# Skip term inside the spectral product, shift inside the first stage of u's transform, and a new order of the work

## The chip, the cores and the metric

The kernel runs on one core of one Trainium2 chip. A core has five engines with an instruction stream each: TensorE (PE in the profile; PEld is its weight load), VectorE (DVE), ScalarE (ACT), GpSimd (POOL) and SyncE (SP). The last two mostly start DMA transfers here. The metric is the device time of one execution in microseconds. Three executions of the kernel before took 679.55, 679.65 and 680.83 us; the median is 679.65 us.

## The reference, cut to what matters

One transformer-like block with adaptive layer norms: 2048 time steps (L) of 512 channels (D). The first half is a state-space convolution (S4), done in the reference by a Fourier transform of length 4096; the second half is a dense layer of 512 to 1792 to 512 with the Mish function.

```python
mod = (_silu(c) @ w_mod).reshape(c.shape[0], 6, 1, -1)
sa, ca, ga, sb, cb, gb = ...
h = _layernorm(x) * (1 + ca) + sa
x = x + ga * S4(h)
h = _layernorm(x) * (1 + cb) + sb
x = x + gb * mlp(h)

# S4(u): K is a kernel of 2048 taps per channel, from the parameters A, B, C, dt
K = einsum("dn,dnl,dn->dl", C, exp(dt * A * l), dt * B).real
y = irfft(rfft(pad(u)) * rfft(pad(K)))[:L] + u * Dskip
```

Two terms are what the change is about: the shift `sa` that is added to the normalised input, and the skip `u * Dskip`.

## The kernel before, in words

The channels are four blocks `b` of 128. Each block has eight steps; a step of the kernel's side has the number `k` = 0 to 31, a step of the spectral side has the number `v` = 0 to 31. Two streams run beside each other and meet in a product.

**The kernel's side** makes K for 16 channels a step and transforms it. Parameters of a block are worked out on VectorE in stages (`params`, called `p0` to `p5` in the plan, tiles `raw` and `pk`). For blocks 1 to 3 the last stage, `p5`, is followed by 48 small DMAs from GpSimd (`load_s`, called `ls`, tiles `s`): 32 for the first half of the block, 16 for the second. From them TensorE makes the coarse exponents (`vt`, tile `pco`) and the angles (`ang`, tile `pang`); ScalarE takes exponentials (`va`, tiles `co`, `cf`) and sines (`sin`, tile `ec`); VectorE multiplies them (`mag`, tile `m`, and `comb`, four instructions on `ec`); TensorE contracts (`kgen`, tile `pkg`, then `ka`, tile `pka`, with ScalarE's copy `ks` between), and ScalarE copies the result to `gk` (`tm`). After eight steps a block's `gk` is whole and the second stage of its transform can be made (`ubk`, tile `pkb`, four products with the table `mf`).

**The input's side** normalises the 2048 rows (tiles `xr`), and makes the first stage of u's transform over 32 time steps at a time (`ua`, eight groups, each 8 products of 32x64 weights `bdu` into four banks `pua`). ScalarE copies the 32 banks to SBUF (`us`), SyncE stores them to DRAM in 64 transfers (`ud`). When all of it is stored, SyncE reads it back in the other layout (`gu`, one transfer a step). Second stage: `ubu` (tile `pub`, the same table `mf`), scaled by ScalarE into `ug` with the gate `gd` (`ug`). VectorE multiplies `pkb` and `ug` into `q` and adds the two halves (`prod`). Back: transpose (`t1`, tile `pt`), inverse second stage (`invb`, tile `pib`), a store and a load through DRAM, inverse first stage (`inva`, tile `pia`), and a VectorE addition onto x (`add`).

**The two terms before.** The shift is constant over time, so it is added to the spectrum as (shift / scale) times the known transform of a constant: one bf16 product `pub<-su,sab` ahead of the four `mf` products in every `ubu` (line 790). `sab` holds the ratio in three bf16 parts that VectorE and ScalarE make in turn from a broadcast (`srt`, `sra`, `srv`). The first `ubu` waits for the third `sra`. The skip is a tap at time zero of K: a product with 4 rows, `pkg<-skip`, after the 32 products of each `kgen` (line 622).

**What sets the order.** Everything from step 2 on is ordered by `_plan` (line 57), a list scheduler that runs while the program is built. Every piece of work is an `op` with an engine, a cost in `NS`, a priority from `LEAD` or `AT`, and the pieces it waits for; TensorE, ScalarE and VectorE then issue in exactly that order (class `InOrder`). A piece that is not ready holds all that stands behind it on its engine. SyncE's and GpSimd's transfers are put in place by the framework, following the same list. PSUM has six single banks that go round (`psum`, tag `pb`) and one double bank for `pang`. The last eight spectral steps stand in `drain()` in an order written by hand, and then comes the dense part.

Of the kernel before, what the change touches and what calls it, by code (L numbers as in the profile page):

```python
# [11 lines left out]
F32 = mybir.dt.float32  # L12
# [27 lines left out]
NS = {"ang": 1400, "sin": 2900, "mag": 1140, "comb": 3570, "kgen": 1130, "ks": 270, "ka": 620, "tm": 560, "ubu": 1410,  # L40
      "ug": 770, "ubk": 1020, "prod": 1760, "t1": 590, "yt": 490, "invb": 1000, "z": 500, "inva": 1060, "add": 1210,
# [4 lines left out]
LEAD = {"ang": -0.94, "sin": -10.68, "mag": 10.1, "comb": 8.65, "kgen": 0.44, "ks": -5.36, "ka": -4.53,  # L46
        "tm": 5.68, "ubu": 7.3, "ug": 3.1, "ubk": 8.28, "prod": 9.39, "t1": 7.94, "yt": 15.87, "invb": 9.41,
        "z": 10.16, "inva": 15.63, "add": 16.89}
AT = {"ua": 1.0, "un": 0.19, "nr": -0.6, "lf": 3.0, "na": 3.0, "sr": 5.0, "st": -0.5, "us": 0.0, "m3": 1,
      "m5": 2, "m0": 3, "p2": -18.07, "p3": -1.69, "pa": -0.41, "p4": -14.88, "p5": -4.69, "ls": 4.36,  # L50
      "p0": -20.55, "p1": -7.87, "v1": -14, "v2": -4.01, "v3": -4.01, "vn": 1.22, "e1": 0, "e2": 0, "e3": 0,
      "m1": 18.57, "m2": 21.11, "m4": 26.23}
# [4 lines left out]
def _plan(k0):  # L57
# [9 lines left out]
    for n, g in enumerate(UO):  # L67
# [3 lines left out]
        op(("ua", g), "T", at, [("nr", g), ("nr", 8 + g)] + ([("ua", UO[n - 1])] if n else []), 4)  # L71
# [5 lines left out]
    for n, i in enumerate((3, 5, 0)):  # L77
        at = AT[f"m{i}"]
        op(("we", i), "S", at - 1, [("mm", (3, 5, 0)[n - 1])] if n else [])
# [4 lines left out]
    op(("sr", 0), "V", AT["sr"], [("mo", i) for i in (3, 5, 0)])  # L84
# [8 lines left out]
    for k in range(max(k0 - 1, 0), nk - 1):  # L93
        op(("kgen", k), "T", lead("kgen", k), [("comb", k), ("ka", k - 1)], 2)
        op(("ks", k), "A", lead("ks", k), [("kgen", k), ("ka", k - 1)])
        op(("ka", k), "T", lead("ka", k), [("ks", k)])
        op(("tm", k), "A", lead("tm", k), [("ka", k)], frees=[("kgen", k)])
# [39 lines left out]
    for n, e, d in (("srt", "T", ("sr", 0)), ("sra", "A", ("srt", 0)), ("srv", "V", ("sra", 0)), ("sra", "A", ("srv", 1)),  # L137
                    ("srv", "V", ("sra", 1)), ("sra", "A", ("srv", 2))):
        i = d[1] + (n == "srv")
        op((n, i), e, AT["sr"], [d, ("prod", -1)], n == "srt", [("srt", 0)] if (n, i) == ("srv", 1) else None)  # L140
# [63 lines left out]
def _constants():  # L204
# [34 lines left out]
    z = np.exp(-2j * np.pi * (4 * np.arange(2048) + 1) / 8192)  # L239
    one = ((1 + 1j) / (1 - z)).reshape(64, 8, 4)  # L240
    one = np.stack([one.real, one.imag]).transpose(2, 0, 3, 1).reshape(4, 2, 512)
    su = np.zeros((4, 32, 2, 512))
    hl = np.zeros((P, 2))
    for e in range(3):
# [3 lines left out]
        for n in range(3):  # L248
            su[:, 3 * n + e] = part
            hl[3 * n + e::32, :n] = -1  # L250
    f = np.float32
    return {
        "su": su.reshape(P, 1024).astype(f),
        "hl": hl.astype(f),
# [14 lines left out]
        "tap": np.eye(4, 4, dtype=f).repeat(32, axis=1) * (np.arange(P) % 32 == 0).astype(f),  # L269
# [19 lines left out]
def s4_block(ctx, tc, io, out):  # L289
# [87 lines left out]
    skip = cst.tile([4, 2, P], F32, name="skip")  # L377
    nc.sync.dma_start(skip[:, 0], io["tap"])
    nc.sync.dma_start(skip[:, 1], io["skip"])
# [1162 lines left out]
```

## Time and profile before

| | |
|---|---|
| median of 3 runs | 679.65 us (679.55 to 680.83) |
| profiled execution, first to last instruction | 686.5 us |
| PE busy | 631.9 us, 92% |
| DVE busy | 475.4 us, 69% |
| ACT busy | 403.8 us, 59% |
| POOL busy | 101.3 us, 15% |
| granted TensorE clock, mean | 0.955 |

The profiled execution is 6.85 us longer than the median of the timed runs; the profile gives its span alone, and no other time of that execution. The profile is of one execution; its stages are: up to about 44 us loads and the first parameters; 44 to 120 us the first stage of u and the first kernel steps; 120 to 320 us the steady part, in which both streams run; 320 to 354 us the drain; then the end of the S4 half and the dense part.

How to read the rows. A row of a timeline has the start, the length, the engine, the source line (almost always 301, a helper through which all work is issued), the operation, `out<-in`, the shape and how many instructions were merged. In brackets stands idle time of the engine just before and what ended it. A row of a group ends with busy time and the mean of one instruction, then idle time before the group's instructions and what ended it. A row of windows has the stretch, its length, and for each engine the busy time in it (with the instructions), then the granted clock, the DMA share and GB/s. A matmul in fp32 shows as two records. The length of a PE row holds the emptying of the array, which the next row overlaps; what a piece costs in a row of work without gaps is the distance from its start to the start of the next.

### The profile page before, as it was taken

Reading aid. Unit: us, or ns where it says so; the run is one execution under the profiler, and the core shown is the slowest. Engines: PE = TensorE matmul, PEld = TensorE weight load, DVE = VectorE, ACT = ScalarE, POOL = GpSimd, SP = SyncE. Lnnn points to the kernel's source line nnn. Section 1 sums busy time; section 2 is a strip of 40 time slices with the busy share of each in tenths; the row PEclk is TensorE's granted clock in tenths of the full one; section 3 lists DMA queues with packets and bytes.
Section 4 is the critical chain, followed back from the end, with each engine's and each line's share of the span. In section 5 each row is a group of like instructions: output and inputs, shape, how many; then the busy total and the mean of one; then the engine's idle time right before and its main releaser. Section 6 shows DMA issues by size and latency. Waiting matters only on the chain.

```text
span 686.5 us, 16596 instructions
## 1 busy us (share of the span) xinstructions
PE 631.9 (92%) x6746; PEld 507.0 (74%) x6746; DVE 475.4 (69%) x903; ACT 403.8 (59%) x707; POOL 101.3 (15%) x212
## 2 busy tenths in 40 slices
PE   0578888999989999999999999999999999999997
PEld 0434465678868677877875888789899899998996
DVE  7988877997499986996766898476336823653233
ACT  3678769867788779876643764453445334534231
POOL 2004413542107240000100000000000001000000
PEclk9958777989999999999999999999999999999999
DMA  9968978422466466555998987667334653373332
GB/s 250 209 228 228 229 182 243 110 63 72 116 181 167 129 186 184 149 150 163 255 269 237 317 277 226 216 172 201 119 92 135 177 151 92 93 215 124 93 93 62
DMA packets 108220, 117.55 MB, mean 171 GB/s; under 512 B 12904, under 2 KB 84976, under 8 KB 106992
## 3 DMA queue, kind: packets, MB, share of 16 engines
q1 hardware_dynamic: 93296, 85.62, 44.1%
q0 software_dynamic: 14464, 30.36, 15.8%
q8 instruction: 53, 0.87, 0.6%
q10 hardware_dynamic: 384, 0.52, 0.3%
q14 instruction: 23, 0.19, 0.1%
HBM read 81.85 MB, written 32.51 MB: 167 GB/s over the span
## 4 chain that ended last, share of the span: by engine, by line
PE 68%; DVE 12%; DMA 9%; ACT 7%; issue 3%; SPq 1%; DVEq 0%; ACTq 0%
PE pr L301 25%; PE pp L301 9%; PE pkg L301 7%; PE pang L301 6%; PE pub L301 5%; PE pib L301 4%; DMA xr<-in_A_u 3%; PE pkb L301 3%; ACT ec L301 2%; PE pt L301 2%; DVE raw L301 2%; DVE ec L301 2%; PE pia L301 2%; DMA w2s<-in_B_w 1%; DVE w L301 1%
## 5 line engine op out<-in xcount | busy, mean ns | idle before, releaser
L301 PE MATMUL pr<-hh,w 128*128 128x256 f32 (+1 forms) x420 | 78.2, 327 | 0.5 <-ACT hh L301 0.5
L301 ACT ACTIVATE ec<-pang 128x1024 f32<-128x1024 f32 x64 | 62.4, 1030 | 25.3 <-PE pang L301 25.3
L301 PEld LDWEIGHTS pr<-hh,w 128*128 128x128 f32 x420 | 66.6, 188 | 12.7 <-ACT hh L301 1.9
L301 DVE TENSOR_TENSOR mh<-x,pr 128x256 f32<-128x256 f32 x63 | 26.4, 419 | 65.2 <-PE pr L301 64.9
L301 PE MATMUL pp<-w,mah 128*128 128x512 f32 x224 | 71.3, 400 | 0.0
L301 PE MATMUL pr<-w,mah 128*128 128x512 f32 x224 | 70.4, 396 | 0.0
L301 DVE TENSOR_TENSOR ec<-ec,m 128x1024 f32<-128x1024 f32 x64 | 61.3, 957 | 9.8 <-ACT ec L301 4.8
L1262 POOL DMA_DIRECT2D w<-w2d x42 | 22.2, 528 | 303.5 <-PE pp L301 197.5
L301 ACT ACTIVATE mh<-mh,b 128x256 f32<-128x256 f32 x63 | 32.1, 510 | 53.2 <-DVE mh L301 52.9
L528 POOL DMA_DIRECT2D s<-pk x96 | 47.4, 500 | 65.2 <-PE pang L301 58.6
L301 ACT ACTIVATE mh<-pr,b 128x256 f32<-128x256 f32 (+1 forms) x35 | 19.4, 559 | 63.0 <-PE pr L301 63.0
L301 DVE TENSOR_TENSOR q<-pkb,ug 128x1024 f32<-128x1024 f32 x32 | 39.1, 1221 | 22.7 <-PE pkb L301 22.5
L301 DVE TENSOR_TENSOR mal<-mh,mah 128x512 fp32r<-128x512 f32 x56 | 38.6, 689 | 15.8 <-ACT mah L301 15.7
L301 DVE TENSOR_TENSOR m<-cf 128x1024 f32<-128x1024 f32 x32 | 39.0, 1218 | 10.2 <-ACT cf L301 10.2
L301 ACT ACTIVATE ug<-pub,gd 128x512 f32<-128x512 f32 x64 | 34.0, 590 | 20.4 <-PE pub L301 20.4
L301 PE MATMUL pr<-w,mal 128*128 128x512 f32 x112 | 44.3, 395 | 0.0
L301 PE MATMUL pp<-w,mal 128*128 128x512 f32 x112 | 44.2, 394 | 0.0
L301 PEld LDWEIGHTS pkg<-ec 128*32 128x32 f32 x2048 | 35.4, 117 | 11.1 <-ACT us L301 4.4
L301 PE MATMUL pkg<-ec 128*32 128x64 f32 x2048 | 40.8, 234 | 3.0 <-ACT us L301 1.9
L301 PEld LDWEIGHTS pp<-w,mah 128*128 128x128 f32 x224 | 38.9, 191 | 5.1
L301 DVE TENSOR_TENSOR x<-x,pr 128x256 f32<-128x256 f32 x42 | 17.6, 419 | 34.3 <-PE pr L301 34.3
L526 POOL DMA_DIRECT2D s<-pk x48 | 23.7, 500 | 108.0 <-ACT ks L301 56.0
(172 smaller groups left out, 1418.2 us busy)
## 6 DMA issues: line engine op xcount, KB each, us to landing
w<-w2d POOLq DMA_DIRECT2D x42, 512.0 KB, 3.6
ud<-us SPq DMA_DIRECT2D x64, 128.0 KB, 2.7
gu<-ud SPq DMA_DIRECT2D x32, 256.0 KB, 3.2
zd<-z SPq DMA_DIRECT2D x32, 256.0 KB, 4.1
zt<-zd SPq DMA_DIRECT2D x32, 256.0 KB, 5.2
w2d<-w SPq DMA_DIRECT2D x14, 512.0 KB, 3.9
xf<-x2d SPq DMA_DIRECT2D x16, 256.0 KB, 4.7
x2d<-xp SPq DMA_DIRECT2D x14, 256.0 KB, 3.1
```

Of the source, the lines that this page charges most:

```text
L301: ins = f(*a, **kw)
L526: nc.gpsimd.dma_start(S3[b, i][q, :], pk[32 * i:32 * i + 32, 8 + k, :])
L528: nc.gpsimd.dma_start(S12[b, g][64 * e + 16 * k:64 * e + 16 * k + 16].rearrange("p h n -> p (h n)"), pk[d, k + 4 * e, :])
L1262: nc.gpsimd.dma_start(t, w2d[f])
```

## The change

1. The skip is added to the spectrum of K inside VectorE's product: `(pkb + skip) * ug`, which needs two instructions of 512 elements where one of 1024 was. The product `pkg<-skip` is gone from all 32 `kgen`. `Dskip` is loaded as 128x4 single numbers.
2. The shift is added in the first stage: the transform over 32 steps of a constant is `cs`, and each `ua` group gets 8 more products `pua<-sab,cs` (32 rows, 64 columns of weights, bf16). The product `pub<-su,sab` is gone from all 32 `ubu`. `sab` now has to be there ahead of the first `ua` instead of the first `ubu`. The ratio is split into three bf16 parts on 128x4 numbers, then broadcast by 16 small bf16 products; two ScalarE copies and two VectorE instructions of 512 elements go.
3. The gate `gd`, which needs the third slice of the modulation, is split off (`gates`, `sg`); the slices 3 and 5 load side by side into different tiles.
4. All priorities in `LEAD` and `AT` are new, and the costs of `kgen`, `ubu`, `ua`, `sra` and `sr`.

```diff
-NS = {... "kgen": 1130, ... "ubu": 1410,
+NS = {... "kgen": 1110, ... "ubu": 1010,
...
-      "sc": 2600, "nr": 450, "ua": 1150, "us": 580, "we": 240, "na": 490, "lf": 60, "sr": 400}
-LEAD = {"ang": -0.94, "sin": -10.68, "mag": 10.1, "comb": 8.65, "kgen": 0.44, "ks": -5.36, "ka": -4.53,
...
+      "sc": 2600, "nr": 450, "ua": 1400, "us": 580, "we": 240, "na": 490, "lf": 60, "sr": 1100, "sg": 200}
+LEAD = {"ang": -1.72, "sin": -14.83, "mag": 4.37, "comb": 8.2, "kgen": 8.11, "ks": 1.94, "ka": -7.81, "tm":
...
-        op(("ua", g), "T", at, [("nr", g), ("nr", 8 + g)] + ([("ua", UO[n - 1])] if n else []), 4)
+        op(("ua", g), "T", at, [("nr", g), ("nr", 8 + g)] + ([("ua", UO[n - 1])] if n else [("sra", 0)]), 4)
...
-    op(("sr", 0), "V", AT["sr"], [("mo", i) for i in (3, 5, 0)])
+    op(("sr", 0), "V", AT["sr"], [("mo", i) for i in (3, 5)])
+    op(("sg", 0), "V", AT["sg"], [("mo", 0), ("sr", 0)])
...
-        op(("ubu", v), "T", lead("ubu", v), [("gl", v, LOAD), ("ug", v - 1), ("t1", v - 2)] + ([("sra", 2)] if v == 0 else []), 1)
-        op(("ug", v), "A", lead("ug", v), [("ubu", v), ("t1", v - 2)], frees=[("ubu", v)])
+        op(("ubu", v), "T", lead("ubu", v), [("gl", v, LOAD), ("ug", v - 1), ("t1", v - 2)], 1)
+        op(("ug", v), "A", lead("ug", v), [("ubu", v), ("t1", v - 2)] + ([("sg", 0)] if v == 0 else []), frees=[("ubu", v)])
...
-        T.matmul(pk[:, 0:256:64], skip[:, 0], skip[:, 1, 4 * k:4 * k + 4], start=False, stop=True, skip_group_check=True)
...
-        w = cv.tile([P, D], F32, tag="gu", name=f"wm{n}", bufs=4)
+        tag = ("us" if k else "xp") if s == 5 else "gu"
+        w = cv.tile([P, D], F32, tag=tag, name=f"wm{n}", bufs={"gu": 4, "us": 3, "xp": 2}[tag])
...
-    def sr_v(n):
-        V.scalar_tensor_tensor(SR1["a"], sab, hl[:, n - 1:n], SR1["a"] if n > 1 else SR1["p"], op0=OP.mult, op1=OP.add)
...
-                T.matmul(ps[a][64 * h:64 * h + 64, :], bdu[r, :], XR[8 * h + g][r, :], start=True, stop=True)
+                T.matmul(ps[a][64 * h:64 * h + 64, :], bdu[r, :], XR[8 * h + g][r, :], start=True, stop=False,
+                         skip_group_check=True)
+        for h in range(2):
+            for a in range(4):
+                r = slice(32 * a, 32 * a + 32)
+                T.matmul(ps[a][64 * h:64 * h + 64, :], cs[r, :], sab[r, :], start=False, stop=True, skip_group_check=True)
...
-        T.matmul(p, sab[g, b * P:b * P + P], su[g, s % 2, :], start=True, stop=False, skip_group_check=True)
-        mf_mm(v, p, lambda r: GU[v][:, r, :], True)
+        mf_mm(v, p, lambda r: GU[v][:, r, :])
...
-        V.tensor_mul(q, kv[:, ::-1, None].to_broadcast([P, 2, 2, 256]),
-                     bass.AP(tensor=u.tensor, offset=u.offset, ap=[u.ap[0], [256, 2], [256, 2], [1, 256]]))
+        V.tensor_mul(q[:, 0], kv[:, 1:2].to_broadcast([P, 2, 256]), u[:, :2])
+        V.scalar_tensor_tensor(q[:, 1], kv[:, 0:1].to_broadcast([P, 2, 256]), skip[:, v // 8:v // 8 + 1], u[:, 1:],
+                               op0=OP.add, op1=OP.mult)
```

The new table says little by itself; three places show what it does. On TensorE in the steady part, in steps of block 0 of the spectral side, the order before is (`gu` is the loaded first stage, `yt` the transposed product):

```order
L301 MATMUL pt_2048<-ident,ug_1902 128x128 x4
L301 MATMUL pkb<-mf,gk_775 128x2x64 x4
L301 LDWEIGHTS sab
L301 MATMUL pub<-su,sab 128x512
L301 MATMUL pub<-mf,gu_1575 128x2x64 x4
L301 MATMUL pib<-yt_2064,mi 128x128 x4
L301 MATMUL pkg<-ec_1835 32x64 x32
L301 MATMUL pkg<-skip 128x4
```

and of the change:

```order
L294 MATMUL pt_2188<-ident,ug_1998 128x128 x4
L294 MATMUL pkb<-mf,gk_614 128x2x64 x4
L294 MATMUL pub<-mf,gu_1786 128x2x64 x4
L294 MATMUL pkg<-ec_1912 32x64 x32
L294 MATMUL pib<-yt_2246,mi 128x128 x4
```

The products with `su` and `skip` are gone, and the second stage of u often stands right behind that of K. On TensorE in the early part, where the modulation slices (`pmodr`, `pmodp`) and the first `ua` group (`pua`) stand, the order before is:

```order
L301 MATMUL pmodr<-wm_418,sc 32x512
L301 MATMUL pua<-xr_146,bdu 64x512 x4
L301 MATMUL pua<-xr_147,bdu 64x512 x4
L301 MATMUL pmodp<-mean,q 128x1 x4
L301 MATMUL pmodr<-wm_477,sc 32x512
```

and of the change, at the first `ua` group:

```order
L294 MATMUL pmodp<-mean,q 128x1 x4
L294 MATMUL pkg<-ec_465 32x64 x32
L294 MATMUL pua<-xr_147,bdu 64x512 x4
L294 MATMUL pua<-xr_148,bdu 64x512 x4
L294 LDWEIGHTS cs
L294 MATMUL pua<-sab,cs 64x512
```

The first `ua` group moved from behind the first modulation slice to behind all three slices, the broadcast of the ratio and the third `kgen` (`ec_465`). On VectorE, the last parameter stage of block 1 (`p5`, the instructions on `raw_83` that end in `pk_421`) before stands between `mag` and `comb` of step 1:

```order
L301 TENSOR_TENSOR m_612<-cf_00_281 128x1024
L301 SCALAR_TENSOR_TENSOR raw_83<-raw_83 128x128 x2
L301 TENSOR_SCALAR raw_83<-raw_83 128x128
L301 SCALAR_TENSOR_TENSOR raw_83<-raw_83 128x128
L301 CAST pk_421<-raw_83 128x6x128
L301 TENSOR_TENSOR pk_421<-raw_83,pk_421 128x6x128
L301 TENSOR_TENSOR ec_406<-ec_406,m_612 128x32x32
```

and of the change, between `mag` and `comb` of step 7, with the stages `p3` and `p4` directly ahead of the rows shown:

```order
L294 SCALAR_TENSOR_TENSOR raw_83<-raw_83 128x128 x3
L294 TENSOR_SCALAR raw_83<-raw_83 128x128
L294 SCALAR_TENSOR_TENSOR raw_83<-raw_83 128x128
L294 CAST pk_430<-raw_83 128x6x128
L294 TENSOR_TENSOR pk_430<-raw_83,pk_430 128x6x128
L294 TENSOR_TENSOR ec_1035<-ec_1035,m_1089 128x32x32
```

The stages `p3`, `p4` and `p5` of block 1 moved behind seven `comb` groups, and with them GpSimd's 32 transfers that read `pk`. For block 2, `p2` now stands just ahead of the first `prod`, and `p3`, `p4` and `p5` behind it; before, all but `p5` were done ahead of the first `ubu`, which comes earlier than the first `prod`.

More of the change, by code (lines that the diff above doesn't have):

```diff
@@ L96, in _plan @@
         op(("ka", k), "T", lead("ka", k), [("ks", k)])
-        op(("tm", k), "A", lead("tm", k), [("ka", k)], frees=[("kgen", k)])
+        op(("tm", k), "A", lead("tm", k), [("ka", k)] + {8: [("ua", UO[-1])], 16: [("ubk", 7)], 24: [("ubk", 15)]}.get(k, []), frees=[("kgen", k)])
     for v in range(nk - 6):
@@ L136, in _plan @@
                frees=[("vt", 4 * b + n)], table="E")
[L137 to L140, printed above, removed]
+    op(("srt", 0), "T", AT["sr"], [("sr", 0)], 1)
+    op(("sra", 0), "A", AT["sr"], [("srt", 0)], frees=[("srt", 0)])
     op(("lm", 0), "P", 8, [("ang", 7), ("us", 31)])
@@ L238, in _constants @@
         mc[2:4, d, x, :32] = 1
[L239 to L243, printed above, removed]
+    one = da.sum(0)
+    cs = np.zeros((P, 64))
     for e in range(3):
@@ L702, in shift_ratio, with gates @@
         V.tensor_add(d, d, gd[:, :NB])
-        V.tensor_mul(gd[:, :NB], modp[:, 0, :], d)
+        V.reciprocal(gd[:, :NB], d)
+        r = modp[:, 5, :]
+        V.tensor_mul(r, r, gd[:, :NB])
+        for n in range(3):
+            V.tensor_copy(parts[:, :, 3 * n:3 * n + 3], r[:, :, None].to_broadcast([P, NB, 3]))
+            if n < 2:
+                V.tensor_sub(r, r, parts[:, :, 3 * n])
+    def gates():
+        V.tensor_mul(gd[:, :NB], modp[:, 0, :], modp[:, 3, :])
         V.tensor_scalar(gd[:, NB:], gd[:, :NB], -1.0, None, op0=OP.mult)
-        V.reciprocal(d, d)
-        V.tensor_mul(modp[:, 5, :], modp[:, 5, :], d)
     SR1 = {}
@@ L712, in sr_t @@
         for b in range(NB):
-            T.matmul(p[:, b * P:b * P + P], modp[:, 5, b:b + 1].to_broadcast([P, P]), ident, start=True, stop=True)
-        SR1["a"] = work().rearrange("p k c x -> p k (c x)")[:, 0]
+            for a in range(4):
+                T.matmul(p[32 * a:32 * a + 32, b * P:b * P + P], parts[:, b, :], identb, start=True, stop=True)
     def sr_a(n):
-        A.copy(sab, SR1["a"] if n else SR1["p"])
-    def sr_v(n):
-        V.scalar_tensor_tensor(SR1["a"], sab, hl[:, n - 1:n], SR1["a"] if n > 1 else SR1["p"], op0=OP.mult, op1=OP.add)
+        A.copy(sab, SR1["p"])
     def rsqrt(dst, var, n, pool, tag, half=True):
@@ L777, in s4_block, with mf_mm @@
     PU, PKB, UG = {}, {}, {}
-    def mf_mm(v, p, lh, started):
+    def mf_mm(v, p, lh):
         s = v % 8
@@ L783, in mf_mm @@
             T.matmul(pv[:, :, r, :], lh(r), mf[:, 4 * s + r, :].rearrange("p (c s) -> p c s", c=2),
-                     start=not started, stop=True, skip_group_check=started)
+                     start=True, stop=True)
     def s_ubu(v):
```

48 lines of the change are left out of this document (21 added, 27 removed), and 5 rows, old and new, of tables (AT, NS).

## The prediction

> **What bounds the kernel now.** I read the page first, then busy time by stretches, then TensorE's timeline in one step of the steady part, then the waits of DVE.
>
> ```profile
> span 686.5 us, 16596 instructions
> PE 631.9 (92%) x6746; PEld 507.0 (74%) x6746; DVE 475.4 (69%) x903; ACT 403.8 (59%) x707; POOL 101.3 (15%) x212
> ```
>
> PE is the busy engine on average, but the dense part, which the change leaves alone, is in that average. So here are stretches of the S4 half (each row: stretch, length, busy us of PE, PEld, DVE, ACT, POOL with instructions, granted clock, DMA share, GB/s):
>
> ```profile
> 30.00:119.90 89.90, 71.77 (x996) 42.47 (x994) 72.19 (x156) 70.77 (x118) 24.75 (x50) 0.73 0.83 220
> 140.00:200.00 60.00, 57.01 (x911) 47.39 (x910) 46.28 (x67) 45.17 (x81) 12.11 (x25) 0.96 0.36 97
> 200.00:254.00 54.00, 53.95 (x995) 40.77 (x994) 51.86 (x62) 40.18 (x68) 23.63 (x48) 0.98 0.66 168
> 254.00:320.00 66.00, 65.30 (x1175) 51.25 (x1172) 56.19 (x62) 54.75 (x95) 0.00 (x0) 1.00 0.61 166
> 320.00:354.00 34.00, 33.03 (x346) 28.06 (x345) 20.23 (x23) 21.09 (x39) 3.35 (x6) 1.00 0.88 247
> ```
>
> The early stretch has slack on every engine: it is bound by chains and loads, and PE stands 18 us. From 140 us on PE is full. But DVE is not far behind: 51.86 of 54 us in the second row, 56.19 of 66 in the third. Whatever PE gains there ends where DVE begins to bind, and I take that at 96%, the densest share that these rows show (51.86/54).
>
> ```profile
> DVE q L301 <- PE pkb L301: 22.5, 13, 6.6
> DVE m L301 <- ACT cf L301: 8.1, 2, 4.2
> ```
>
> DVE's idle time from 128 to 354 us (sum in us, count, longest) is mostly `prod` waiting for PE's `pkb`. That is the room which a shorter PE stream can use.
>
> **The change part by part.** First what leaves PE:
>
> ```profile
> 207.65 1.06 PE L301 MATMUL pkb<-mf,gk 128*128 128x128 f32 x8
> 208.63 0.50 PE L301 MATMUL pang<-ah,s 64*128 64x256 f32 x4
> ...
> 210.05 0.39 PE L301 MATMUL pub<-su,sab 32*128 32x512 bf16 x1
> 210.36 1.16 PE L301 MATMUL pub<-mf,gu 128*128 128x128 f32 x8
> 211.56 1.16 PE L301 MATMUL pkg<-ec 128*32 128x64 f32 x64
> 212.65 0.38 PE L301 MATMUL pkg<-skip 4*128 4x4 f32 x2
> 212.96 1.16 PE L301 MATMUL pib<-yt,mi 128*128 128x128 f32 x8
> ```
>
> ```profile
> L301 PE MATMUL pub<-su,sab 32*128 32x512 bf16 x30 | 12.0, 399 | 0.0
> L301 PE MATMUL pkg<-skip 4*128 4x4 f32 x46 | 8.7, 258 | 0.0
> ```
>
> From start to start the shift product takes 210.36 - 210.05 = 0.31 us and the skip product 212.96 - 212.65 = 0.31 us. The groups are of 128 to 354 us: 30 shift products, and 46 skip records, which are 23 products. So (30 + 23) x 0.31 = 16.4 us of PE time go. The lowest price I allow is half, 0.15 us each or 8 us, if the next group pays part of the refill anyway.
>
> The eight `mf` records behind the shift product take 211.56 - 210.36 = 1.20 us, where the same eight behind `pib` take 208.63 - 207.65 = 0.98. The Trainium skill, "TensorEngine Tiling (Array Packing)", Tiling Modes, Key Properties, states that changing the tiling mode drains TensorE. The rows agree in direction, since the shift product uses 32 rows and `mf` 128. By that rule up to 30 x 0.11 = 3.3 us more would be freed (half the difference, as `mf` often follows another mode still), of which DVE's limit below would leave about 1.
>
> Second, what PE gets: eight products `pua<-sab,cs` for each of eight `ua` groups, which no row shows. Nearest are a group's own products:
>
> ```profile
> 72.23 1.11 PE L301 MATMUL pua<-xr,bdu 32*64 32x512 f32 x16
> ```
>
> Those are 16 records in 1.11 us, so eight bf16 records of the same shape would be 0.55; the upper bound is 1.11 and the lower 0.25 (less than one shift product, if the 32x64 pieces overlap). I take 0.5, so 8 x 0.5 = 4 us (2 to 9). They lie in the first stretch, where PE stands 18 us; that idle time hides them, and without it they would cost the 4 us.
>
> Third, VectorE's product is now two instructions of 512 in place of one of 1024:
>
> ```profile
> 136.55 1.22 DVE L301 TENSOR_TENSOR q<-pkb,ug 128x1024 f32<-128x1024 f32 x1
> 137.80 0.69 DVE L301 TENSOR_TENSOR ug<-q 128x512 f32<-128x512 f32 x1
> 138.41 1.22 DVE L301 TENSOR_TENSOR m<-cf 128x1024 f32<-128x1024 f32 x1
> ...
> L301 DVE TENSOR_TENSOR xp<-xp,pia 128x512 f32<-128x512 f32 x8 | 5.1, 684 | 0.6 <-PE pia L301 0.6
> ...
> 108.92 0.75 DVE L301 SCALAR_TENSOR_TENSOR q<-sab,hl,pmod 128x512 f32<-128x512 bf16 x1 [1.52 <-ACT sab L301]
> ```
>
> Now it is 1.25 us from start to start. A 512 instruction takes 0.61 (137.80 to 138.41); one out of PSUM lasts 0.684 like the 0.69 of the one just timed; a three-operand one lasted 0.75. Two of them are 1.22 to 1.39, so the split costs -0.03 to 0.14; I take 0.07, or 32 x 0.07 = 2.2 us, half of it where DVE sets the pace.
>
> Fourth, parameters. The stages `p3` to `p5` of block 2 move from ahead of the first `prod` to behind it, and `p2` just ahead of it. Their work is in one stretch before (columns here: DVE, ACT, clock, DMA share, GB/s; only instructions on `raw`):
>
> ```profile
> 112.50:128.00 15.50, 8.88 (x29) 0.62 (x2) 0.84 0.49 163
> ```
>
> So DVE in the stretch from 140 to 200 gets about 8.9 us more on 46.28, which is 55.2.
>
> **The sum by stretches, bound by DVE at 96%.** In 140 to 200, 55.2 / 0.96 = 57.5, so 2.5 us can go, less the split: 2. In 200 to 254, DVE is at the limit: 0. In 254 to 320, 56.19 / 0.96 = 58.5 allows 7.5, but PE frees only about 4.8 (some 8 steps of 0.62): 4.8. In 320 to 354, DVE is far off; 7 shift and 1 skip products of 0.31 are 2.5. Together 9.3. From that I take 1 for the split, 1 for friction (PE in order and at most 96% where both are dense), and 1.5 for the start, which follows. That leaves 5.8, say 6 us.
>
> **The start.** The first `prod` needs `ubu` 0 (DRAM copy of `ua` and block 0's `gk`). Before:
>
> ```profile
> 41.69 0.18 DVE L301 SCALAR_TENSOR_TENSOR nmr<-mv,rstd 128x16 f32<-128x16 f32 x1
> ...
> 61.14 1.94 DVE L301 TENSOR_TENSOR ec<-ec,m 128x1024 f32<-128x1024 f32 x2
> ...
> 64.74 1.22 DVE L301 TENSOR_TENSOR m<-cf 128x1024 f32<-128x1024 f32 x1
> 65.99 1.22 DVE L301 TENSOR_TENSOR ec<-ec,m 128x1024 f32<-128x1024 f32 x1
> ```
>
> ```profile
> 103.92 0.51 PE L301 MATMUL pang<-ah,s 64*128 64x256 f32 x4
> ...
> 119.91 0.39 PE L301 MATMUL pub<-su,sab 32*128 32x512 bf16 x1
> ```
>
> ```profile
> 60.85 3.92 POOL L526 DMA_DIRECT2D s<-pk  x8 [56.02 <-ACT ks L301]
> ...
> 77.30 1.00 POOL L528 DMA_DIRECT2D s<-pk  x2
> ```
>
> ```profile
> s<-pk POOLq DMA_DIRECT2D x144, 16.0 KB, 3.0
> gu<-ud SPq DMA_DIRECT2D x32, 256.0 KB, 3.2
> ```
>
> ```profile
> 94.88 7.67 SPq L769 DMA_DIRECT2D ud<-us  x10
> ```
>
> The 32 transfers of `ls` start at 60.85 and end at 78.3, 17.45 us, and land 3.0 later. In the change they wait for `p5` of block 1, which stands behind seven `comb`. A `comb` is 64.74 - 61.14 = 3.60 us, a `mag` 1.25. Seven of each are 34; with `p3` to `p5` (three quarters of the 8.88 above, 6.7) and small work that is some 45 us of DVE; from about 42 us, where the row of the norms (`nmr`) frees DVE for steps, and with waits for ACT, `p5` ends at 92 to 95. Then 17.45 + 3.0 gives 112 to 115 for the first `pang` out of `s`, where it was 103.92. Before, 119.91 - 103.92 = 16 us lay between that `pang` and the first `ubu`. In the change `kgen` 7 and `ka` 7 are ahead of `ubu` 0, and only sines (3 us) and the exponentials stand between, so I put `ubu` 0 at 124 to 125. The other way to it, the 64 stores of `us`, moves as well: `ua` waits for the modulation and the broadcast, and SyncE needs 7.67 / 10 = 0.77 us a store; 64 are 49 us from about 67, ending near 116, and landing of `gu` makes 116 to 125. Both ways agree on 118 to 131 as bounds. That is 5 us later for `ubu` 0, but its `ubk` and `prod` follow at once (129, where `prod` was at 136.55), so the later start costs 1.5 us (a third of 4.6 us, the part of that work which is not done earlier on PE instead); bounds are -4 and +8.
>
> **The rivals.** R1: all the PE time is kept, 16.4 less 1.5 or 15 us. For it: PE is full from 140 on, and DVE has 22.5 + 8.1 us of waits, more than 16.4. Against it: the 51.86 of 54 in the second stretch, and 8.9 us more of parameters. Span 671.5.
>
> R2: nothing is left; the 0.31 us were mostly refill which the next product pays, half the PE time (8 us) is gone, and DVE eats that with the split and the later parameters. For it: DVE's 96%. Against it: in 254 to 354 DVE has room. Span within 1.4 us of before (0.2%, about what a measurement of this kernel can tell from no change).
>
> R3, slower: PE stands ahead of the first `pang` of block 1, in order, while the POOL transfers (behind `p5`) have not landed; `ubu`, `ubk` and everything of the spectral side are queued behind it on PE. What such an idle time does shows earlier in the run:
>
> ```profile
> 35.76 1.22 PE L301 MATMUL pang<-early,s 128*128 128x256 f32 x4 [5.63 <-ACT ec L301]
> ...
> 32.00:36.00 4.00, 0.24 (x1) 0.24 (x2) 3.69 (x14) 3.94 (x6) 0.00 (x0) 0.50 0.86 247
> 44.00:48.00 4.00, 3.77 (x19) 0.69 (x17) 3.86 (x14) 3.49 (x4) 0.00 (x0) 0.50 0.11 22
> ```
>
> PE stood 5.63 us and the granted clock was 0.50, still so at 44 to 48 us. An idle time of that size at 112 us and some 8 us of half clock behind it cost 5.6 + 4, about 9.6, against the 5.8 gained: 4 us slower, span 690.5. It decides from a first `ubu` at about 131 us on. Against it: PE has `ua` and `kgen` work of block 0 to do meanwhile. The Trainium skill, "TensorE: Matmul & The Clock Gate", HAM oscillation, says that idle gaps over about 3.4 us bring the clock down again; the rows agree with a gap of 5.63 us and a clock of 0.50.
>
> **How the numbers follow.** The profiled execution is 686.5 us and the median 679.65, so 6.85 us are taken off each span. Forecast: 686.5 - 6 = 680.5, median 673.6 us, own range 669 to 677, chance 0.46. R1: 664.6, 0.21. R2: about 679.6, 0.12. R3: 683.6, 0.21. All best bounds together give -16 (663.6), the start's upper bound +5 (684.6); the range is 664 to 684. Faster 0.46 + 0.21 = 0.67, same 0.12, slower 0.21.
>
> **What would show it.** Right: PE has no `pub<-su` and no skip group; the new `pua` group has 4 to 8 us busy; the first `pub` is at 118 to 131 us; DVE's wait for `pkb` falls from 22.5 to about 8 to 10 us; DVE is at 93% or more between 140 and 300; `q` shows two rows of about 0.68 us; the dense part begins about 6 us earlier. R1 would show the same wait falling with DVE well under 93%. R2 would show DVE full and the steps of `mf` behind another mode still slow. R3 would show PE idle for several us ahead of `pang<-ah` and a granted clock near 0.50 there. The forecast is wrong if the steady part is no shorter, or if its gain is lost ahead of the first `pub`.

## The result and the profile after

| | before | changed |
|---|---|---|
| median | 680.24 us (679.55 to 681.91, 4 runs) | 706.8 us (703.75 to 707.84, 4 runs) |
| ratio to before, 95% interval | | 1.0332 (1.0284 to 1.0381) |
| profiled execution, span | 686.5 us | 706.1 us |
| start of the dense part in it | 372.7 us | 396.3 us |

The change is 3.3% slower; 673.6 us were forecast, and at most 684. The medians differ by 26.6 us, the spans by only 19.6, since the profiled execution before was a long one: the dense part, which has the same 1770 TensorE instructions in both, took 313.9 us in it and 309.9 in this one, and times that are compared between two traces carry such differences of a few us. The S4 half ends 23.6 us later, and that is where to look.

The page of the changed kernel:

```profile
span 706.1 us, 16609 instructions
PE 616.7 (87%) x6722; PEld 497.4 (70%) x6722; DVE 478.5 (68%) x938; ACT 402.7 (57%) x705; POOL 102.0 (14%) x214
```

TensorE did lose work: 631.9 us busy before, 616.7 now. The time came as idle time. Busy time by stretches, first of the kernel before, then of the changed one (stretch, length, busy PE, PEld, DVE, ACT, POOL, granted clock, DMA share, GB/s):

```profile
100.00:140.00 40.00, 34.31 (x651) 25.25 (x650) 32.29 (x61) 36.01 (x61) 20.44 (x42) 0.84 0.62 168
240.00:280.00 40.00, 39.53 (x718) 30.79 (x718) 31.51 (x35) 33.46 (x59) 7.84 (x16) 1.00 0.72 192
```

```profile
100.00:140.00 40.00, 23.11 (x262) 14.54 (x263) 12.46 (x30) 20.65 (x37) 19.87 (x40) 0.70 0.84 227
240.00:280.00 40.00, 33.12 (x514) 24.55 (x513) 29.24 (x39) 23.61 (x38) 23.72 (x48) 0.87 0.66 173
```

Two places stand out. Between 100 and 140 us all three compute engines idle at once: VectorE has 12.46 us of work where it had 32.29, at a clock of 0.70. And around 260 us TensorE, full before, falls to 33 of 40 us with the clock at 0.87. GpSimd is busy for half of both stretches, in the second for 23.7 us where it was 7.8. Waits of TensorE and of VectorE in the changed kernel from 90 to 300 us (sum, count, longest):

```profile
PE pang L294 <- DMA s<-pk: 12.0, 4, 6.2
PE pub L294 <- issue: 9.8, 1, 9.8
```

```profile
DVE m L294 <- ACT cf L294: 16.4, 3, 15.6
DVE raw L294 <- ACT raw L294: 12.6, 2, 9.0
```

Before, TensorE waited for neither, and VectorE's longest wait for `cf` was 4.2 us. TensorE now waits for the parameter transfers `s<-pk` of GpSimd; the wait put down to "issue" is the one for the first `gu`. The first place, on TensorE, SyncE and GpSimd:

```profile
107.72 0.39 PE L294 MATMUL pang<-ah,s 64*128 64x256 f32 x2
114.29 0.97 PE L294 MATMUL pang<-ah,s 64*128 64x256 f32 x2 [6.18 <-DMA s<-pk]
...
122.17 3.23 PE L294 MATMUL pco<-mc,s 128*128 128x512 f32 x8
135.17 2.04 PE L294 MATMUL pub<-mf,gu 128*128 128x128 f32 x8 [9.78 <-issue]
```

```profile
114.86 8.73 SPq L773 DMA_DIRECT2D ud<-us  x12
123.65 2.75 SPq L390 DMA_DIRECT2D xp<-in_A_u  x3
132.35 2.04 SPq L779 DMA_DIRECT2D gu<-ud  x4
```

```profile
111.77 8.33 POOL L520 DMA_DIRECT2D s<-pk  x17
...
120.58 1.12 POOL L989 DMA_DIRECT2D mi<-in_mi  x2
```

TensorE stands 6.18 us before the second half of its first `pang` of block 1, and 9.78 us before the first `pub`. SyncE issues the last store at 123.6 us, yet the first `gu` only at 132.35: it waits until the stores have landed, and beside the last of them run two loads of 1 MB (`mi`), which GpSimd issued at 120.58, right after its transfers. Landing of a store takes 2.9 us in the median here; the last three, issued from 120.9 us on, took 10.1 to 10.8. The second place, the start of block 3, on VectorE, GpSimd and TensorE:

```profile
240.04 0.96 DVE L294 TENSOR_TENSOR pk<-raw,pk 128x768 fp32r<-128x768 f32 x1
```

```profile
240.56 1.02 POOL L518 DMA_DIRECT2D s<-pk  x2 [44.10 <-PE pub L294]
...
258.49 3.57 POOL L520 DMA_DIRECT2D s<-pk  x7
```

```profile
261.16 0.35 PE L294 MATMUL pang<-ah,s 64*128 64x256 f32 x1 [3.21 <-DMA s<-pk]
263.35 2.07 PE L294 MATMUL pib<-yt,mi 128*128 128x128 f32 x8
```

The last parameter stage ends at 241.0 us (206.86 + 0.96 = 207.8 before); the transfers follow at once, half a microsecond each, and TensorE, in order, waits for them. Behind the wait an inverse stage takes 2.07 us from record to end where others take 1.06 to 1.16: the clock has dropped. How far it drops shows in the changed kernel first, then in a run of it without this wait (the one with six transfers, below), behind the same place in the order:

```profile
258.00:262.00 4.00, 0.65 (x4) 0.38 (x5) 2.75 (x3) 0.80 (x3) 3.88 (x9) 1.00 0.64 142
264.00:272.00 8.00, 8.00 (x93) 7.61 (x93) 4.99 (x7) 3.28 (x5) 3.44 (x8) 0.50 0.35 78
```

```profile
256.00:264.00 8.00, 8.00 (x156) 6.10 (x156) 6.45 (x10) 6.31 (x11) 0.00 (x0) 1.00 0.59 159
```

After a wait of 3.2 us TensorE runs 8 us at 0.50, so such a wait costs more than its own length. From the start of the 14th product to that of the 16th the changed kernel needs 31.6 us, the run without the wait 23.0. Block 2 has a wait of 2.4 us of the same kind at 188 us; between the 7th product and the 8th the changed kernel loses 4.3 us against that run.

### The profile page after: what moved, and what is told of

It is laid out like the page before. It is cut to its first block, busy times and chain, and to the rows that moved or that the text cites. A ratio compares the mean times of both kernels' runs of the same rounds, so it can differ in the third digit from the quotient of the medians.

```text
span 706.1 us, 16609 instructions
## 1 busy us (share of the span) xinstructions
PE 616.7 (87%) x6722; PEld 497.4 (70%) x6722; DVE 478.5 (68%) x938; ACT 402.7 (57%) x705; POOL 102.0 (14%) x214
## 4 chain that ended last, share of the span: by engine, by line
PE 55%; DMA 13%; DVE 10%; issue 9%; ACT 7%; POOL 4%; SPq 1%; DVEq 0%; ACTq 0%; POOLq 0%
PE pr L294 31%; PE pp L294 11%; DVE ec L294 4%; DMA s<-pk 4%; ACT ec L294 3%; PE pang L294 3%; DMA zt<-zd 3%; DMA xr<-in_A_u 2%; POOL s L518 2%; PE pkg L294 2%; POOL s L520 2%; DVE q L294 2%; DMA zd<-z 2%; PE pib L294 1%; PE pia L294 1%
## 5 line engine op out<-in xcount | busy, mean ns | idle before, releaser
L294 DVE TENSOR_TENSOR m<-cf 128x1024 f32<-128x1024 f32 x32 | 38.9, 1217 | 16.4 <-ACT cf L294 16.4
L294 PE MATMUL pub<-mf,gu 128*128 128x128 f32 x256 | 37.8, 294 | 10.4 <-issue 9.8
L294 PEld LDWEIGHTS pub<-mf,gu 128*128 128x128 f32 x256 | 33.6, 204 | 13.0 <-issue 11.3
```

The costliest lines, as they stand in the source:

```text
L294: ins = f(*a, **kw)
```

## The experiments

Theories: O, the new order costs and the arithmetic is good; A, the arithmetic hurts; M, the `mi` load collides with the last stores; L, the parameters and their transfers are late; S, u's first stage, late since it needs the shift ratio, makes its stores late. Ratios are to the kernel before, in runs on the same chip, with 95% intervals; 0.1% is 0.7 us. On the chips of these runs the kernel before took 682 to 684 us in the median, so times are compared by the ratio.

**Skip alone, old order.** The edits of point 1 of the change on the kernel before; nothing else.

```diff
-        T.matmul(pk[:, 0:256:64], skip[:, 0], skip[:, 1, 4 * k:4 * k + 4], start=False, stop=True, ...)
...
-        V.tensor_mul(q, kv[:, ::-1, None]..., ...)
+        V.tensor_mul(q[:, 0], kv[:, 1:2].to_broadcast([P, 2, 256]), u[:, :2])
+        V.scalar_tensor_tensor(q[:, 1], kv[:, 0:1].to_broadcast([P, 2, 256]), skip[:, v // 8:v // 8 + 1], u[:, 1:], ...)
```

> The kernel before with only the skip term moved into VectorE's product; the order of all work is the old one. If the arithmetic is good and the new order is what costs (theory O, order), this is no slower than before: 32 x 0.31 = 10 us of TensorE time go and 2 us of VectorE time come, 670 to 680 us. If the split product itself hurts (theory A, arithmetic), it is slower than 682 us, since VectorE is at 96% from 200 to 254 us.

Measured: 679.43 us, ratio 0.9948 (0.9918 to 0.9977). Faster by 0.5%: theory A falls for this half, and theory O stands.

**Shift left out, old order.** The 32 shift products of the kernel before are dropped.

```diff
-        T.matmul(p, sab[g, b * P:b * P + P], su[g, s % 2, :], start=True, stop=False, skip_group_check=True)
-        mf_mm(v, p, lambda r: GU[v][:, r, :], True)
+        mf_mm(v, p, lambda r: GU[v][:, r, :], False)
```

> The kernel before without the 32 products of the shift (the shift is left out of the result), in the old order, which still has everything that makes the ratio. It is the most that taking these products off TensorE can bring there. If TensorE's time is worth what my sum said (30 x 0.31 = 9.3 us freed, a third to a half of it kept), 675 to 677 us; if VectorE takes it all, 679 to 681; if the change of array shape costs more than the 0.31 us, below 672.

Measured: 676.1 us, ratio 0.9857 (0.9824 to 0.9889): about 10 us by the ratio. The time itself lies in the first expected range, but the kernel before took 684.2 us on this chip; by the ratio the gain is that of the third. The stretch from the first to the last product, in the kernel before, with the skip moved, and with the shift left out:

```profile
137.80:353.30 215.50, 209.96 (x3418) 168.23 (x3418) 175.99 (x211) 163.38 (x285) 41.29 (x84) 0.98 0.59 158
```

```profile
138.70:350.20 211.50, 202.60 (x3375) 160.54 (x3375) 179.19 (x243) 163.96 (x285) 42.20 (x85) 0.98 0.61 162
```

```profile
136.00:342.60 206.60, 195.74 (x3388) 163.37 (x3388) 175.31 (x211) 163.14 (x284) 41.10 (x83) 0.98 0.60 163
```

TensorE loses 7.4 us by the skip, and 4.0 of them leave the stretch, while VectorE gets 3.2 more. It loses 14.2 us by the shift, and 8.9 leave. Those 14.2 are more than the products' own time, 32 times 0.31 us. The groups of the `mf` products of `pub`, of the kernel before and without the shift (128 to 354 us):

```profile
L301 PE MATMUL pub<-mf,gu 128*128 128x128 f32 x240 | 36.5, 298 | 0.0
```

```profile
L301 PE MATMUL pub<-mf,gu 128*128 128x128 f32 x240 | 33.2, 283 | 0.2 <-ACT yt L301 0.2
```

The same 240 records take 3.3 us less without the 32-row product ahead of them, 0.11 us for each of 30. The Trainium skill ("TensorEngine Tiling (Array Packing)", Tiling Modes, Key Properties: a change of tiling mode drains the array) agrees with this row. No run shows that the drain is the reason. The prediction had worked out 3.3 us by it from another pair of rows, and had left it out of its sum.

**The `mi` load ahead of the transfers**, in the changed kernel:

```diff
-    op(("lm", 0), "P", 8, [("ang", 7), ("us", 31)])
+    op(("lm", 0), "P", 8, [("ang", 7)])
...
-            after(nc.gpsimd.dma_start(MI[0][...], io["mi"][...]), US["last"].ins)
+            nc.gpsimd.dma_start(MI[0][...], io["mi"][...])
```

> The changed kernel, same order on TensorE, VectorE and ScalarE; only the 2 MB load of the inverse table (mi) is issued by GpSimd ahead of the 32 parameter transfers, right after the last angles of block 0 at about 84 us, where it was issued at 120.6 us, in the same microseconds as the last stores of u's first stage. Theory M (collision): the last store then lands about 126 us where it landed about 132, the first gu load is issued 5 to 7 us earlier and the time falls by 4 to 8 us, to 699 to 703. If the late parameters alone decide (theory L), the first angles of block 1 still come at 114 to 121 us and the time stays within 2 us of 706.8.

Measured: 699.62 us, ratio 1.0257 (1.0212 to 1.0302). SyncE in it:

```profile
114.47 6.00 SPq L773 DMA_DIRECT2D ud<-us  x9
120.53 1.57 SPq L390 DMA_DIRECT2D xp<-in_A_u  x3
122.33 2.04 SPq L779 DMA_DIRECT2D gu<-ud  x4
```

From the last store's issue to the first `gu` it is now 1.9 us, where it was 8.8. Theory M holds for its part; 2.6% remain.

**Six transfers of parameters in place of 32**, in the changed kernel and in the one before (and two in place of the 16 of the second half). The sorting of rows is left out, so K comes from other parameters; all instructions stay:

```diff
-            for k in range(4):
-                ... 2 or 4 transfers of 16 KB
+            if half == 0:
+                for i in (g, g + 1):
+                    nc.gpsimd.dma_start(S3[b, i], pk[:, 8, :])
+            nc.gpsimd.dma_start(S12[b, g]..., pk[:, 0:2, :]...)
```

> The changed kernel with the 32 parameter transfers of a half block replaced by 6 of the same bytes (wrong rows are read, so the K side is computed from wrong parameters; all instructions stay). GpSimd then needs about 3 us where it needed 17. Theory L (late parameters, transfers priced too low by the order): the angles of block 1 come at about 101 us instead of 114 to 121, those of block 3 at about 248 instead of 261, and the time falls by 10 to 18 us, to 689 to 697. Theory S (the shift ahead of u's first stage makes the stores late): the first gu load stays at about 126 to 132 us, the loss at the start stays, and only the 6 us ahead of block 3 come back: about 700.

> The kernel before with the same replacement (wrong rows, K side from wrong parameters). Theory L: the old order leaves room for the transfers (they end at 78 us and are used at 104), so the time is within 3 us of 680. If the transfers are a cost of either order, it falls by 5 us or more.

Measured: changed kernel 688.75 us, ratio 1.0118 (1.0041 to 1.0194); kernel before 683.12 us, ratio 1.0029 (1.0001 to 1.0058). So the transfers cost the new order about 2.1%, give or take 0.8, and the old one nothing. The shorter queue also brings the `mi` load forward, from 120.58 to 98.64 us, so this run and the one before it do not cut wholly different things. GpSimd at block 3 of the first:

```profile
234.63 1.05 POOL L516 DMA_DIRECT2D s<-pk  x2 [55.58 <-PE pub L294]
...
237.32 0.53 POOL L517 DMA_DIRECT2D s<-pk  x1
```

One number was missed: the angles of block 1 came at 116 us, not 101, since TensorE stood in its order behind the last `ua` groups. The first product moved by 1.6 us (141.8 to 140.2 us, its last instruction), but the 8th by 5.9, the 15th by 11.9 (272.0 to 260.1) and the 19th by 17.1: the gain lies for the most part at the starts of blocks 2 and 3, in the waits and the low clock behind them. Of the last 5.2 us, 2.6 come between the 18th product and the 19th, where no wait for a transfer stands; the run with the load moved does not lose them there, and their cause is open.

**Both cuts.** The edits of the last two together.

> The changed kernel with both cuts at once: the 2 MB load ahead of the parameter transfers, and 6 parameter transfers in place of 32 (wrong rows, K side from wrong parameters). The single cuts gave 7.2 and 18.1 us. If they hit different places (the collision only the first gu load, the transfers the starts of blocks 2 and 3), they add up: 706.8 - 25.3 = 681.5, within 3. If both shorten the same start, about 688. What is then left against the 670 to 674 that were forecast for the whole change is neither the collision nor the transfers.

Measured: 683.77 us, ratio 0.9993 (0.9964 to 1.0023). They add up within the intervals (0.75% and 2.1% alone, 3.4% together), and the kernel is back at the time before, not below it. Something still eats the gain.

**Stores of u's first stage from a second queue.** First from ScalarE, in the kernel with the load moved and in the one with both cuts:

```diff
-            US["last"] = nc.sync.dma_start(view(ud, ...
+            US["last"] = (nc.scalar if h and p >= 16 else nc.sync).dma_start(view(ud, ...
```

> The changed kernel with the 2 MB load moved (as in the run that gave 699.6 us), and the second half of the last 16 banks of u's first stage stored from ScalarE's queue, so that SyncE issues 48 transfers where it issued 64. Order as before on all engines. Theory S (the stores, started late, hold up ScalarE's copies, and behind them TensorE and the K side): the last store goes out 5 to 10 us earlier, about 112, the first gu load at about 115, VectorE has over 16 us of work between 100 and 134 us where it had 11.4 in the changed kernel, and the time falls by 4 to 8 us, to 692 to 696. If the transfers of parameters set that place too, the time stays within 2 us of 699.6.

> The same with 6 parameter transfers in place of 32 (wrong rows, K side from wrong parameters): all three causes cut. The two cuts alone left the kernel at the time of the one before (ratio 0.9993). Theory S: the remaining gain comes out, 6 to 12 us below that, ratio 0.982 to 0.991. If the stores were no cause, the ratio stays within 0.997 to 1.002.

Measured: 701.55 us, ratio 1.0302 (1.0263 to 1.0340), and 685.74 us, 1.0070 (1.0045 to 1.0095). Both somewhat slower, and neither tells of theory S, because ScalarE now pays for the issues. ScalarE in the first of them:

```profile
106.86 0.59 ACT L294 COPY us<-pua 128x512 f32<-128x512 f32 x1 [1.28 <-DMA ud<-us]
107.51 0.58 ACTq L773 DMA_DIRECT2D ud<-us  x1
108.13 0.59 ACT L294 COPY us<-pua 128x512 f32<-128x512 f32 x1 [0.41 <-ACT ks L294]
108.75 0.61 ACTq L773 DMA_DIRECT2D ud<-us  x1
```

Each issue holds ScalarE for 0.6 us, as long as the copy itself, and the last store still goes out at 119.2 us. So the same with GpSimd's queue, which is mostly idle in the kernel with both cuts, and for the last 24 banks:

```diff
-            US["last"] = nc.sync.dma_start(view(ud, ...
+            US["last"] = (nc.gpsimd if h and p >= 8 else nc.sync).dma_start(view(ud, ...
```

> The changed kernel with the load moved and 6 parameter transfers in place of 32 (ratio 0.9993 so far), and the second half of the last 24 banks of u's first stage stored from GpSimd's queue, which is idle there now, where ScalarE paid 0.61 us for each issue in the try before. Theory S: SyncE has 40 stores in place of 64, the last one goes out at about 110 us in place of 122, the first gu load at about 113, VectorE's wait for the exponentials of block 1 (11.5 us, ending at 119.6) falls by 5 us or more, and the ratio comes to 0.982 to 0.992. If the stores are no cause, the wait and the ratio (0.996 to 1.003) stay.

Measured: 676.81 us, ratio 0.9890 (0.9853 to 0.9928). SyncE and the stretch from first to last product, with both cuts and then with the stores shared:

```profile
101.60 20.52 SPq L769 DMA_DIRECT2D ud<-us  x30
...
123.97 2.04 SPq L775 DMA_DIRECT2D gu<-ud  x4
...
134.10:350.40 216.30, 196.82 (x3517) 160.84 (x3517) 194.26 (x271) 174.58 (x302) 11.71 (x22) 0.99 0.58 163
```

```profile
98.77 12.95 SPq L769 DMA_DIRECT2D ud<-us  x12
...
116.41 2.04 SPq L775 DMA_DIRECT2D gu<-ud  x4
...
126.10:342.40 216.30, 195.61 (x3517) 159.53 (x3518) 194.25 (x273) 174.61 (x303) 11.79 (x22) 1.00 0.59 163
```

The first `gu` comes 7.6 us earlier, the first and the last product 8.0 us earlier, and the stretch between them is the same to a hundredth: 216.30. Theory S holds in that the late stores are a pure shift of everything behind them, worth 1.0%. That they are late because u's first stage needs the ratio was not tested: its first store goes out 8 us later than before (67.99 us in the changed kernel, 59.90 before), its last one 21 us later. The way was not quite as expected: VectorE's long wait for the exponentials did not shrink (11.5 us, then 13.2), it came earlier, and TensorE's wait of 4.9 us for the first `gu` behind it went.

The same rows say that the steady part gained nothing: 216.3 us from first to last product, 215.5 before. TensorE has 13 us less work in it, and VectorE 194.3 us where it had 176.0.

**A third table of priorities.** The whole change with the `mi` load moved, and the table chosen by a search through the kernel's own list scheduler with the transfers at the price that the trace gives (17.45 us); on the skip alone, the same kind of search.

```diff
-      ... "ls": 9000, ...
+      ... "ls": 17500, ...
-LEAD = {...}
-AT = {...}
+LEAD = {"ang": 5, "sin": 13.95, "mag": -5.99, ...}
+AT = {"ua": -41.89, "un": 14.44, "nr": -35.18, ...}
```

> The whole change with the 2 MB load moved and a third table of priorities, chosen with the 32 transfers priced at 17.5 us in the plan where it had 9. If the price was the fault of the new order (theory L), the arithmetic of the change now shows its gain: 668 to 677 us, and the angles of blocks 1, 2 and 3 wait for the transfers for less than 1 us each. If the late stores (theory S) cost by themselves, about 682 or more.

> Only the skip term moved, with a table of priorities chosen the same way. The old order did not depend on the price of the transfers, so little is to be had: 676 to 680 us. If it comes out as fast as the whole change with its new table, the shift in the first stage of u brings nothing.

Measured: 679.02 us, ratio 0.9914 (0.9875 to 0.9953), and 683.24 us, 0.9995 (0.9958 to 1.0032). The whole change is now faster than the kernel before in this one measurement of 6 executions; its `pang` no longer waits for a transfer of parameters between 90 and 300 us. The new table for the skip alone came out above its expectation, and is no gain over the old one (0.9948).

> The whole change with the third table (ratio 0.9914), and 6 parameter transfers in place of 32 (wrong rows, K side from wrong parameters). Theory L: this order has room for the 32 transfers, so the ratio stays within 0.987 to 0.995, where the same cut took 18 us off the changed kernel. If the transfers cost in any order, it falls below 0.985.

Measured, with the six transfers on top: 678.86 us, ratio 0.9962 (0.9923 to 1.0000). That is just above the expected 0.987 to 0.995. No gain: in this order the transfers are hidden, as in the old one.

**Whole kernels with shared stores.** Third table, 16 stores from ScalarE or from GpSimd; and the skip alone with 16 from GpSimd (the edit as above, from bank 16 on).

> The whole change with the third table of priorities (ratio 0.9914 so far), and the same 16 stores from ScalarE's queue. Theory S: u's first stage is late there too (last store at 121.9 us), so another 3 to 6 us come, ratio 0.982 to 0.988. If ScalarE pays for the issues what SyncE saves, the ratio stays at 0.990 to 0.995.

> A whole kernel with everything that the runs point to: the change, the 2 MB load moved, the third table of priorities, and the second half of the last 16 banks stored from GpSimd's queue once it has issued the parameter transfers of block 1. Theory S: the last store goes out about 8 us earlier than 121.9, and the first product with it; ratio 0.980 to 0.986, the fastest whole kernel of this study. If GpSimd's queue holds the stores back behind its transfers, 0.990 to 0.996.

> Only the skip term moved, old order (ratio 0.9948), and the same 16 stores from GpSimd's queue. In the old order u's first stage starts 18 us earlier and the last store goes out at 104 us with the first product waiting for the K side as well, so theory S expects no more than 2 us: ratio 0.992 to 0.996. If the stores bind the old order too, 0.98 to 0.99.

Measured: 684.0 us, 1.0031 (0.9994 to 1.0069); 683.02 us, 0.9998 (0.9966 to 1.0030); 680.25 us, 0.9957 (0.9924 to 0.9989). The last store goes out at 121.2 and 121.6 us in the first two, as late as without the edit (121.9). With GpSimd's queue its stores stand among its parameter transfers and the `mi` load, and SyncE stands 8.5 us ahead of a load of `xp` until stores have landed, with its own last three stores behind that load. By the ratio both lose what the third table had gained, but their traces do not show it: the dense part starts at 369.4 and 368.1 us, without the edit at 369.2. So the 0.9% of the third table is not beyond doubt, and the 1.0% of theory S is shown in the kernel with six transfers alone; a whole kernel that has it was not found. In the old order the edit brings nothing, as theory S expected, though the last store goes out 4 us earlier.

## Why the prediction was wrong

The forecast was faster by 6 us; it is slower by 26.6. Two steps failed. The larger is the sum by stretches, which was to save 9.3 us from 140 us on: it counted the late parameters as 8.9 us of VectorE's work and the transfers behind them, at blocks 2 and 3, as nothing. The other is the start ("the later start costs 1.5 us"), which left out the `mi` load and put the last store too early. Where each cut acts shows in the ends of the first and the last product:

| run | first product | last product | between |
|---|---|---|---|
| before | 137.8 us | 353.3 us | 215.5 us |
| changed | 141.8 | 374.7 | 232.9 |
| `mi` load moved | 132.5 | 365.7 | 233.2 |
| six transfers | 140.2 | 356.9 | 216.7 |
| both | 134.1 | 350.4 | 216.3 |
| both, stores shared with GpSimd | 126.1 | 342.4 | 216.3 |

The stretch between is 17.4 us longer, and six transfers take back 16.2 of it; the load and the stores move the first product and leave the stretch as it is. The rival R3 (slower, chance 0.21) had the right mechanism, TensorE standing in order ahead of `pang` and a halved clock behind it, and with 9.6 us about the right price for one such wait (8.6 us at block 3). It looked for it at block 1 alone, where the wait of 6.2 us came but where six transfers, which take that wait away, moved the first product by only 1.6 us. That R3 had the sign right is therefore partly luck. Step by step:

- *What leaves TensorE*: 0.31 us a product was right (0.31 or 0.32 for nearly all shift products of the traces), the longer `mf` groups came on top for the shift. Of TensorE's freed time 54% (skip) and 63% (shift) left the stretch in the old order; the sum had 9.3 of 16.4 us, 57%. By the runs with the old order the two edits are worth 0.5% and up to 1.4%, so for that order this half of the sum was too low, not too high.
- *The split product*: 1.38 us from start to start (rows below), so 0.13 a product, at the upper end of -0.03 to 0.14.

```profile
140.43 0.69 DVE L294 TENSOR_TENSOR q<-pkb,ug 128x512 f32<-128x512 f32 x1
141.04 0.74 DVE L294 SCALAR_TENSOR_TENSOR q<-pkb,skip,ug 128x512 f32<-128x512 f32 x1
141.81 0.69 DVE L294 TENSOR_TENSOR ug<-q 128x512 f32<-128x512 f32 x1
...
L294 PE MATMUL pua<-sab,cs 32*64 32x512 bf16 x64 | 8.5, 464 | 0.0
```

- *The products with `cs`*: 8.5 us busy as a group, just above the 4 to 8 that were named as the sign.
- *VectorE's share*: the limit by VectorE was the right idea and its size was too small. Its work between first and last product rose by 194.4 - 176.0 = 18.4 us. By tile, in that stretch, before and then in the changed kernel, in this order `raw` (columns DVE, ACT), `ec` and `q` (PE, PEld, DVE, ACT, or without ACT):

```profile
137.80:353.30 215.50, 8.80 (x29) 0.97 (x3) 0.98 0.59 158
137.80:353.30 215.50, 26.07 (x1408) 22.55 (x1408) 76.68 (x84) 58.56 (x60) 0.98 0.59 158
137.80:353.30 215.50, 0.00 (x0) 0.00 (x0) 59.31 (x62) 0.00 (x0) 0.98 0.59 158
```

```profile
141.80:374.70 232.90, 15.47 (x49) 1.34 (x4) 0.97 0.56 152
141.80:374.70 232.90, 27.99 (x1472) 24.35 (x1472) 84.00 (x92) 66.85 (x68) 0.97 0.56 152
141.80:374.70 232.90, 0.00 (x0) 0.00 (x0) 63.09 (x93) 0.00 (x0) 0.97 0.56 152
```

  Parameters 6.7 us (8.9 were counted), the split product 3.8 (2.2), and 7.3 for two `comb`, which were not counted: the K side is two steps further back at the first product, with both cuts too (84.0 us of `ec`). With both cuts VectorE is busy for 150.9 of the 160 us from 140 to 300, 94%, and its wait for `pkb` in the stretch is down to 5.9 us from 22.5, the two signs that were named for its limit. That this work is why both cuts only came back to the time before is argued from these figures; no run takes it away.
- *The parameters of block 1*: `p5` was put at 92 to 95 us and ended at 95.3; the first `pang` was put at 112 to 115, and its second half came at 114.29. Right. The idle engines ahead of it were not priced: TensorE stood 6.2 us and VectorE 15.6.
- *The stores*: put at about 116 us, the last one went out at 123.6 (the 64 issues took 0.81 us each where 0.77 was counted, and two loads and short waits in between were not), and with the `mi` load beside it the landing was some 7 us late. That load was nowhere in the prediction, though its place in GpSimd's queue, right behind the transfers whose delay I had worked out, makes it late by as much. The first `pub` came at 135.17 us, outside 118 to 131. By the runs, the collision costs 0.75%, the late stores 1.0%.
- *The later blocks*: the prediction priced the 32 transfers for block 1 only. The same lateness recurs at blocks 2 and 3, where `p5` also stands later and TensorE is otherwise full; six transfers in place of 32 gave 2.1%, mostly there. This is the largest term, and it was left at zero without a reason.
- *The sum itself*: the split was taken off twice (in the stretch from 140 to 200 us and once more at the end), and the start has +8 us as its bound in one place and +5 in the range. Neither changes the outcome.
- *The clock*: it was 0.70 from 100 to 140 us, around the waits of 6.2 and 9.8 us, and 0.50 behind the wait of 3.2 us at block 3. The Trainium skill ("TensorE: Matmul & The Clock Gate", HAM oscillation) sets the limit at idle gaps over about 3.4 us. The first two gaps agree; the third is a little shorter and lowered the clock all the same, and here the measurement decides.

In sum of ratios: 1.0332 falls by 3.4% with the collision and the transfers cut, and by another 1.0% with the stores shared, to 0.9890. That this is near the 0.991 that was forecast is luck: the forecast had a shorter steady part and a start that costs 1.5 us, and in this run the steady part is no shorter and the whole gain is a first product 11.7 us earlier.

## What to carry to other kernels

When an order moves a late stage of a producer, follow every queue behind it to its end, for each block in which it recurs, and ask what else stands in that queue: here 32 small transfers and a 2 MB load. Check a planner's price of a transfer against the trace before trusting the order it finds: `ls` was 9 us in the plan and 17.45 in the rows, harmless in an order with slack and 2% in one without. Price a wait of TensorE with the slow clock behind it, not by its length alone. And before moving a term to an earlier stage, ask what the earlier stage was early for.

## What the runs showed of the hardware

- A store of 128 KB that lands in 2.9 us in the median took up to 10.8 us while two loads of 1 MB from another queue were under way. With the loads moved to 82.6 us, the stores beside them took up to 8.7 us and those after 100 us at most 5.2.
- A DMA issue took 0.61 us on ScalarE, where it held the engine as long as the copy it followed; 0.50 (parameters) to 0.66 (stores) on GpSimd; 0.60 in the median on SyncE (stores).
- A 32-row bf16 product between 128-row fp32 ones costs TensorE 0.31 us from start to start and 0.11 more in the eight records behind it.
- A wait of TensorE of 3.2 us was followed by 8 us at a granted clock of 0.50; the run without the wait had 1.00 there.
